# Contiguous key loads, copies on two engines and a join by channel halves in the first stages of a long-convolution kernel

## The chip, the cores and the metric

One Trainium2 chip, one core. The metric is the device time of one execution in microseconds, as the median of several runs of the same program. Engines: TensorE (PE) multiplies matrices into PSUM, VectorE (DVE), ScalarE (ACT) and GpSimd (POOL) work on SBUF (and, here, the first two on PSUM), SyncE (SP) issues most of the DMAs. All arithmetic is in f32.

## The reference

```python
def _A_ref(q, k, v, shift_k, ssm_k, ssm_D):       # S = 2048, D = 448, ks = 4
    k_shift = sum(k_pad[:, t:t + S, :] * shift_k[:, ks - 1 - t] for t in range(ks))
    kv = k_shift * v
    y = causal_conv(kv, ssm_k) + kv * ssm_D       # per channel, 2048 long, by FFT
    return q * y
...
mod = (_silu(c) @ w_mod).reshape(c.shape[0], 6, 1, -1)
sa, ca, ga, sb, cb, gb = ...
h = _layernorm(x) * (1 + ca) + sa
x = x + ga * _A_ref(h, A_k, A_v, A_shift_k, A_ssm_k, A_ssm_D)
h = _layernorm(x) * (1 + cb) + sb
x = x + gb * (sigmoid(h @ w_gate) * (h @ w_up)) @ w_down
```

What matters here is the first half: the short convolution of k with four taps, its product with v, and the long convolution by a Fourier transform written as matrix products. The second half, a gated feed-forward layer, takes the larger part of the time and is not touched.

## The kernel before

The 2048 positions lie as 128 partitions by 16 groups (g), the 448 channels as two halves (h) of 224, or as four blocks (ct) of 112 where the channels lie on the partitions. The order of the instructions on each engine is the order of the program text (a manual schedule). Every engine works off its own queue in order, and waits only for data and for buffers.

**First stage of the kernels** (`stage1_k`, L197 to L207). For half h and load i (four groups), two PSUM tiles (e = 1, then e = 0), each filled by eight matmuls and copied to SBUF (`ak[h]`, 128x896 at a time) by ScalarE. The PSUM tiles come from the tag "t", of which there are two buffers. A few warm-up matmuls go ahead (L572, L573). When half 0 is done, VectorE transposes it in eight steps (`turn`, L181); half 1 goes to DRAM and comes back in another order (`turn_out` L189, `turn_in` L192).

**Second stage of the kernels** (`stage2_k`, L298): eight steps n for half 0, with ScalarE copying out.

**The taps.** `ktl` holds k with the channels on the partitions. Its 16 units (i, ct) each take a tile of 112 x 512. A unit is done in one of three ways: `conv_first` (first product on ScalarE) with three `conv_tap` on VectorE (33 in all); `conv_products` (four products on ScalarE, added by the matmuls that transpose them); or with diagonal matrices on TensorE alone (unit (0,2)). `conv_turn` (L265) transposes a unit into PSUM, in the tags "sa" and "y" (one buffer each), and `conv_mul` (L280) multiplies v by it, in place. The sums of `conv_first` are in the tag "accs", three buffers.

**First stage of kv** (`stage1_v` L209 per group, `stage1_v_half` L223 per half and two groups): matmuls with the same table `zc`, copied to `av[0]` and `av[1]`. Groups 0 to 11 go whole (two copies of 128x448), groups 12 to 15 by halves. For groups 10 and 11, VectorE copies half 1 (L219). When all groups of half 0 are there, VectorE transposes `av[0]` step by step (L183), and the loop `stage2_v` (L318) begins: matmuls, a multiply by the kernels (L332), matmuls back (L349). Between its steps, `beside` (L726) puts the layer norm, the modulation and the second half's kernel stage.

**Loads.** All on SP's queue, in program order. The order is: tables and kernels, `ktl` in 4 + 8 parts (`load_k`, L149), v, the trips of `ak[1]`, then at L683 to L696 two `turn_in`, `mod_load(1)` (L409: two loads of `wmod`, into `spare`, that is the tile `wb`, where groups 8 to 11 of v lie until `stage1_v` has read them), `load_x(0)` and the other `turn_in`. The pool `pk` (with `ktl` and the taps' tiles) is closed at L687, and the pools of x1 and of the "eights" take its place.

Of the kernel before, what the change touches and what calls it, by code (L numbers as in the profile page):

```python
# [10 lines left out]
F32 = mybir.dt.float32  # L11
F32R = mybir.dt.float32r
AF = mybir.ActivationFunctionType
OP = mybir.AluOpType
# [3 lines left out]
P = 128  # L18
C = 224
DT = 112  # L20
NG = 16
# [58 lines left out]
def adaln_conv_glu_kernel(ctx: ExitStack, tc: tile.TileContext, q, kT, v, ssm, shift, dskip,  # L80
                          wgu, wd, cvec, wmod, c1t, w2t, wat, wbt, out):
    nc = tc.nc
    PE, ACT, DVE, POOL = nc.tensor, nc.scalar, nc.vector, nc.gpsimd
# [8 lines left out]
    pk = pk_.enter_context(tc.tile_pool(name="pk", bufs=1, side="right"))  # L92
    ps = ctx.enter_context(tc.tile_pool(name="ps", bufs=1, space=PSUM))
    pd = ctx.enter_context(tc.tile_pool(name="pd", bufs=1, space=bass.MemoryType.DRAM))
    late = {}

    def two(tag, name):

        return ps.tile([P, 2, 512], F32, tag=tag, bufs=2 if tag == "t" else 1, name=name)

    def rows(t):
        return t[:, :, :D]
# [44 lines left out]
        nc.sync.dma_start(xin["v", k], v[:, 2 * k:2 * k + 2])  # L147

    def load_k(ct, part):  # L149
        nc.sync.dma_start(ktl[:, ct, part], kT[:, ct, part])  # L150

    def load_c1(g0, g1):
        nc.sync.dma_start(zc[:, g0:g1], c1t[:, g0:g1])
# [25 lines left out]
    ak = {}  # L179
    
    def turn(a, i):  # L181
        x = a[:, :, i * 28:(i + 1) * 28].rearrange("q p c -> q c p")
        DVE.transpose(x, x)  # L183
# [8 lines left out]
    def turn_in(a, scratch, q, bs=range(4)):  # L192
        x = scratch.rearrange("(b q) p c -> b p q c", b=4)
        for b in bs:
            nc.sync.dma_start(a[32 * b:32 * b + 32, q], x[b, :, q])

    def stage1_k(h, i):  # L197
        x = xin.pop((h, i))
        d = ak[h].rearrange("p (s j) c -> p s (j c)", s=2)
        for e in (1, 0):  # L200
            pt = two("t", f"s1k{h}_{i}_{e}")
            g = 4 * i + 2 * e
            for jj in range(2):
                for s in range(2):
                    r = slice(64 * s, 64 * s + 64)
                    PE.matmul(pt[:, s, jj * C:jj * C + C], zc[r, g + jj], x[r, 2 * e + jj], start=True, stop=True)
            ACT.activation(d[:, :, g * C:(g + 2) * C], rows(pt), AF.Copy)  # L207

    def stage1_v(g):  # L209

        x = xin["v", g // 2][:, g % 2]
        pt = two("t", f"s1v{g}")
        for s in range(2):
            r = slice(64 * s, 64 * s + 64)
            PE.matmul(pt[:, s, :D], zc[r, g], x[r], start=True, stop=True)
        for h in range(2):
            a, y = av[h].rearrange("p (s j) c -> p s j c", s=2)[:, :, g], pt[:, :, h * C:h * C + C]
            if h and g > 9:
                DVE.tensor_copy(a, y)  # L219
            else:  # L220
                ACT.activation(a, y, AF.Copy)

    def stage1_v_half(h, g):  # L223

        pt = two("t", f"s1v{g}_{h}")
        for j in range(2):
            x = xin["v", g // 2][:, j, h * C:h * C + C]
            for s in range(2):
                r = slice(64 * s, 64 * s + 64)
                PE.matmul(pt[:, s, j * C:j * C + C], zc[r, g + j], x[r], start=True, stop=True)  # L230
        d = av[h].rearrange("p (s j) c -> p s (j c)", s=2)
        ACT.activation(d[:, :, g * C:(g + 2) * C], rows(pt), AF.Copy)  # L232

    acc = {}

    def conv_first(i, ct):

        acc[i, ct] = [pk.tile([DT, 4, P], F32, tag="accs", bufs=3, name=f"acc{i}_{ct}")]
        ACT.activation(acc[i, ct][0], ktl[:, ct, 4 * i + 3:4 * i + 7], AF.Copy, scale=sk[:, ct, 0:1])

    def conv_tap(i, ct, tap):
# [6 lines left out]
    def conv_rest(*its):  # L248

        for tap in range(1, 4):  # L250
            for i, ct in its:
                conv_tap(i, ct, tap)

    def conv_products(i, ct):

        acc[i, ct] = []
        for tap in range(4):
            x = ktl[:, ct, 4 * i + 3 - tap:4 * i + 7 - tap]
            a = x if tap == 3 else pk.tile([DT, 4, P], F32, tag="accp", bufs=6, name=f"acp{i}_{tap}")
            ACT.activation(a, x, AF.Copy, scale=sk[:, ct, tap:tap + 1])  # L260
            acc[i, ct].append(a)

    kvs = {}
# [1 line left out]
    def conv_turn(i, *cts):  # L265

        for e in range(2):
            if (i, e) not in kvs:
                kvs[i, e] = two(("sa", "y")[e], f"kv{i}{e}")
            for ct in cts:  # L270
                for g in range(2):
                    y = kvs[i, e][:, g, ct * DT:ct * DT + DT]
                    if (i, ct) not in acc:
                        for tap in range(4):
                            PE.matmul(y, ktl[:, ct, 4 * i + 3 - tap + 2 * e + g], diag[:, tap], start=tap == 0, stop=tap == 3)
                        continue
                    for k, a in enumerate(acc[i, ct]):
                        PE.matmul(y, a[:, 2 * e + g], ident[:DT, :DT], start=k == 0, stop=k == len(acc[i, ct]) - 1, is_transpose=True)

    def conv_mul(i, unit=None):  # L280
        for e in range(2):
            if unit:
                conv_tap(*unit, 2 * e + 1)
                if e == 0:
                    pass
            x = xin["v", 2 * i + e]
            DVE.tensor_mul(x, x, rows(kvs[i, e]))
            if unit and not e:
                conv_tap(*unit, 2)
# [49 lines left out]
    def stage2_back(between=None):  # L339
        h, n, m = products.pop(0)  # L340
        straight = n > (3 if h else 5)
        pt = two("t" if h and n == 7 else "sa", f"sa{h}_{n}")
        for b in range(2):
            if b and between:
                between()
            for ex in range(2):
                r = slice(64 * ex, 64 * ex + 64)
                y = pt[r, b, :D] if not straight else pt[r, b].rearrange("p (j c) -> p j c", c=32)[:, :, :28]
                PE.matmul(y, wa[:, b, r], m[b][:, ex], start=True, stop=True)  # L349
        if straight:  # L350
            y = pt.rearrange("p b (j c) -> p (b j) c", c=32)[:, :, :28]
            DVE.transpose(av[h][:, :, 28 * n:28 * n + 28].rearrange("q p c -> q c p"), y.rearrange("q p c -> q c p"))
            return
        if eights(h, n):
            x = late["pe"].tile([P, 8, DT], F32, name=f"eight{n}")
            late["eights"].append(x)
            x = x.rearrange("p (b j) c -> p b j c", b=2)
        else:
            x = block(av[h], h, n)
        ACT.activation(x, cols4(rows(pt), h, n), AF.Copy)  # L360
# [48 lines left out]
    def mod_load(m):  # L409

        for h in range(2):
            if m != 1:
                wm = quad(*{3: ("m", 4), 4: ("wm", 2), 5: ("wm", 2)}.get(m, ("in", 4)), f"wm{m}{h}")[:DT]
            else:
                wm = spare[:DT, h * 4 * C:(h + 1) * 4 * C].rearrange("p (a c) -> p a c", c=C)
            nc.sync.dma_start(wm, wmod[:, m, h])
            wms[m, h] = wm

# [150 lines left out]
    ordered = tc.manual_schedule()  # L569
    ordered.__enter__()  # L570
    pt = two("y", "warm")
    for i in range(10):  # L572
        PE.matmul(pt[:, 0, :P], ones, ones, start=True, stop=True)  # L573
    for x in (slice(2, 4), slice(0, 2)):
        load_c1(x.start, x.stop)
# [13 lines left out]
    for i in range(4):  # L589
        load_ssm(1, i)  # L590
    nc.sync.dma_start(w2, w2t)
    for ct in (0, 2, 1, 3):
        load_k(ct, ka)
    for h in range(2):
        ak[h] = big.tile([P, 32, C], F32, tag=f"k{h}", name=f"ak{h}")
# [2 lines left out]
    taps = [(i, ct) for i in range(4) for ct in (2, 3)]  # L598
    for k in range(8):
        turn(ak[0], k)  # L600
    for i in range(4):
        stage1_k(1, i)
        load_v(i)
        if i in (1, 3):
            for ct in (0, 2, 1, 3):
                load_k(ct, kb[i // 2])
# [9 lines left out]
    def s1v(*gs):  # L616
        for g in gs:
            stage1_v(g)

    for n in range(8):  # L620
        stage2_k(0, n, "t")
        if n in (0, 1):
            conv_first(0, n)
        if n == 3:
            conv_first(1, 0)
            conv_products(0, 3)
            conv_rest((0, 0), (0, 1))
            conv_turn(0, 2)
        if n == 5:
            conv_first(1, 1)  # L630
            conv_products(1, 2)
            conv_turn(0, 3)
    conv_first(1, 3)
# [42 lines left out]
    for t in (1, 2, 3):  # L676
        conv_tap(3, 3, t)
    conv_turn(3, 2, 0, 1)
    s1v(8, 9)
    conv_turn(3, 3)  # L680
    conv_mul(3)
    s1v(10, 11)
    turn_in(ak[1], kd, slice(0, 8), range(2))  # L683
    mod_load(1)
    if "x" == "y":
        turn_in(ak[1], kd, slice(0, 8), range(2, 4))
    pk_.close()  # L687
    late["px"] = ctx.enter_context(tc.tile_pool(name="px", bufs=1, side="right"))
    late["x1"] = x1 = late["px"].tile([P, NG, D], F32, name="x1")
    pe_ = ExitStack()  # L690
    late["pe"], late["eights"] = pe_.enter_context(tc.tile_pool(name="pe", bufs=1, side="right")), []
    load_x = lambda i: nc.sync.dma_start(x1[:, 4 * i:4 * i + 4], q[:, 4 * i:4 * i + 4])
    load_x(0)
    if "x" != "y":
        turn_in(ak[1], kd, slice(0, 8), range(2, 4))
    turn_in(ak[1], kd, slice(8, 16))  # L696
    for h in range(2):
        for g in (12, 14):
            stage1_v_half(h, g)
        if not h:  # L700
            mod_parts(0, "sa", gbrow)
    pz_.close()
# [722 lines left out]
```

## Time and profile before

| | |
|---|---|
| median of 3 runs | 563.62 us (563.37 to 564.16) |
| profiled execution | 561.75 us |
| its span, first to last instruction | 560.0 us |
| busy: PE / DVE / ACT / POOL | 544.2 / 443.0 / 281.5 / 57.6 us |
| DMA | 107.74 MB, 192 GB/s in the mean |
| granted TensorE clock | 1.0 |

A profile row of the timeline reads: start, time taken, engine, line of the kernel, operation, what it writes <- what it reads, the shape (partitions x elements), how often; in brackets the idle time of the engine ahead of it and what ended it. A row of a stretch gives its length, the busy time of each engine with the number of instructions, the granted clock, the mean busy share of the DMA engines and the rate in GB/s.

### The profile page before, as it was taken

To read this page: it belongs to the slowest core of one execution; us is meant where nothing else is said; L and a number is where in the kernel's file an instruction comes from. 1 tells how busy PE (TensorE), PEld (TensorE's weight loads), DVE (VectorE), ACT (ScalarE), POOL (GpSimd) and SP (SyncE) were. 2 spreads that over 40 slices of the span, in tenths; PEclk is the share of its full clock that TensorE was granted. 3 is DMA by queue.
4 is the path that set the end of the run, shared out by engine and by line. 5 is a ranking of instruction groups with operands and counts; after the bars stand their busy time and mean duration, and the time that the engine had idled before them with its cause. 6 is when DMAs were issued, how large, how long until landed. Compare 5 with 4: busy or idle time off the path is not lost.

```text
span 560.0 us, 7828 instructions
## 1 busy us (share of the span) xinstructions
PE 544.2 (97%) x3010; PEld 415.4 (74%) x3010; DVE 443.0 (79%) x529; ACT 281.5 (50%) x492; POOL 57.6 (10%) x52
## 2 busy tenths in 40 slices
PE   7988899999999999999999999999999999999997
PEld 6564532333577888888888888888888888888886
DVE  0899799989899888898998888885555556879565
ACT  4898688983577586276556452422222222334120
POOL 1000006969500000000000000000000000000000
PEclk9999999999999999999999999999999999999999
DMA  8999899897730408395968295776464662220103
GB/s 278 266 275 391 226 255 288 214 233 159 191 109 0 164 1 322 150 367 187 361 236 307 77 366 162 244 254 240 126 209 135 198 219 105 75 104 8 59 0 132
DMA packets 46953, 107.74 MB, mean 192 GB/s; under 512 B 20034, under 2 KB 25284, under 8 KB 45892
## 3 DMA queue, kind: packets, MB, share of 16 engines
q1 hardware_dynamic: 40468, 82.34, 49.6%
q10 hardware_dynamic: 6448, 24.90, 11.3%
q8 instruction: 24, 0.39, 0.3%
q14 instruction: 13, 0.11, 0.1%
HBM read 70.92 MB, written 35.78 MB: 191 GB/s over the span
## 4 chain that ended last, share of the span: by engine, by line
PE 74%; DMA 10%; DVE 9%; ACT 5%; issue 2%; SPq 0%; DVEq 0%; ACTq 0%
PE d L987 23%; PE b L953 16%; PE c L953 10%; PE a L953 10%; PE gu L1076 4%; DMA kT<-in_kT_dram 4%; PE s2v L328 3%; PE sa L349 2%; PE y L385 2%; DVE av L183 2%; DVE m L332 2%; DMA kdk<-ak 2%; DMA wb<-in_v_dram 1%; DMA inb<-in_ssm_dram 1%; DMA ak<-kdk 1%
## 5 line engine op out<-in xcount | busy, mean ns | idle before, releaser
L987 PE MATMUL d<-wd,h 128*128 128x448 f32 x666 | 144.4, 366 | 0.6 <-DVE wd L547 0.5
L987 PEld LDWEIGHTS d<-wd,h 128*128 128x128 f32 x666 | 124.7, 188 | 13.5 <-DVE wd L547 1.4
L953 PE MATMUL b<-xt,ring 128*128 128x512 f32 x408 | 99.0, 391 | 0.0
L953 PEld LDWEIGHTS b<-xt,ring 128*128 128x128 f32 x408 | 76.5, 188 | 14.9
L1002 DVE TENSOR_TENSOR x<-x,d 128x896 f32<-128x896 f32 x55 | 59.5, 1084 | 16.6 <-PE d L987 16.5
L953 PE MATMUL a<-x,ring 128*128 128x512 f32 x264 | 63.7, 389 | 0.0
L953 PEld LDWEIGHTS a<-x,ring 128*128 128x128 f32 x264 | 49.6, 188 | 10.3
L962 ACT ACTIVATE h<-st 128x512 fp32r<-128x512 f32 x55 | 34.6, 629 | 31.3 <-DVE st L971 19.0
L965 DVE TENSOR_TENSOR h<-st,h 128x512 fp32r<-128x512 f32 x55 | 37.8, 687 | 12.5 <-ACT h L962 12.2
L968 ACT ACTIVATE st<-st 128x512 f32<-128x512 f32 x24 | 15.2, 632 | 63.8 <-DVE st L1313 36.0
L1076 PE MATMUL gu<-x,ring 128*128 128x512 f32 x176 | 42.5, 395 | 0.1
L1267 ACT ACTIVATE st<-st 128x512 f32<-128x512 f32 x12 | 7.6, 631 | 68.0 <-DVE st L1266 68.0
L1076 PEld LDWEIGHTS gu<-x,ring 128*128 128x128 f32 x176 | 32.7, 188 | 7.6 <-issue 0.7
L332 DVE TENSOR_TENSOR m<-s2v,ak 128x896 f32<-128x896 f32 x32 | 33.2, 1078 | 3.9 <-PE s2v L328 2.7
L183 DVE STREAM_TRANSPOSE av<-av 128x896 f32<-128x896 f32 x18 | 33.1, 1874 | 2.4 <-ACT av L232 2.4
L953 PE MATMUL c<-x,ring 128*128 128x512 f32 x144 | 34.8, 390 | 0.0
L934 ACT ACTIVATE ring<-sum 128x512 fp32r<-128x512 f32 x28 | 17.2, 625 | 31.7 <-DVE sum L915 16.8
L328 PE MATMUL s2v<-av,w 64*64 64x448 f32 x256 | 31.8, 546 | 1.0 <-DVE av L183 0.5
L953 PEld LDWEIGHTS c<-x,ring 128*128 128x128 f32 x144 | 27.0, 188 | 5.2
L953 PE MATMUL c<-xt,ring 128*128 128x512 f32 x120 | 29.2, 389 | 0.0
L349 PE MATMUL sa<-m,wa 128*64 128x448 f32 x128 | 27.4, 552 | 0.1
L953 PEld LDWEIGHTS c<-xt,ring 128*128 128x128 f32 x120 | 22.5, 188 | 4.6
(191 smaller groups left out, 778.4 us busy)
## 6 DMA issues: line engine op xcount, KB each, us to landing
fd<-ring ACTq DMA_DIRECT2D x35, 512.0 KB
ring<-fd SPq DMA_DIRECT2D x35, 512.0 KB
wdk<-wd ACTq DMA_DIRECT2D x7, 896.0 KB
wd<-wdk SPq DMA_DIRECT2D x7, 896.0 KB
inb<-in_wgu_dram SPq DMA_DIRECT2D x6, 1024.0 KB
kdk<-ak SPq DMA_DIRECT2D x4, 896.0 KB
ak<-kdk SPq DMA_DIRECT2D x16, 224.0 KB
x<-in_q_dram SPq DMA_DIRECT2D x4, 896.0 KB
```

The source lines that it names most:

```text
L183: DVE.transpose(x, x)
L328: PE.matmul(pts[b][c:c + 64, ex, :D], w2[r:r + 64, ex], x[r:r + 64, b], start=True, stop=True)
L332: DVE.tensor_mul(cols4(m[b], h, n), cols4(rows(pts[b]), h, n), k[:, b].unsqueeze(1).to_broadcast([P, 2, D // w, w]))
L349: PE.matmul(y, wa[:, b, r], m[b][:, ex], start=True, stop=True)
L934: ACT.activation(forms[name, i][:, 0], w_src(name), AF.Copy)
L953: PE.matmul(pt, wh(s, t), x[:, k], start=start and m == 0, stop=stop and m == len(ops) - 1, skip_group_check=True)
L962: ACT.activation(hh, h, AF.Copy)
L965: DVE.tensor_sub(hl, h, hh)
L968: ACT.activation(y[:, 0], y[:, 0], AF.Sigmoid)
L987: PE.matmul(y, h[:, (2 * e + i) * P:(2 * e + i + 1) * P], x, start=m == 0, stop=m == len(ops) - 1)
L1002: DVE.tensor_add(y, y, rows(pt))
L1076: PE.matmul(pt[:, g], plain(q, t)[:, s, g, f * P:f * P + P], xf[xs_[b]][:, k], start=m == 0, stop=m == 10, skip_group_check=True)
```

## The change

- `kT` is laid out in DRAM so that each part that one DMA loads (a block ct, groups 0 to 10, 11 to 14 or 15 to 18) is one contiguous piece; before, each partition's part was a piece of a longer row. The order of the first four blocks is 3, 2, 0, 1 for 0, 2, 1, 3.
- Half 0 of `stage1_k`: the copies of e = 0 go to VectorE. The warm-up has 7 products for 10.
- The four products of unit (0,3) go to GpSimd, issued ahead of everything else there; `conv_first(1,1)` moves ahead from step 5 to step 3; `conv_turn(0,2)` from step 3 to step 4; "accs" has four buffers.
- The join of the taps and of the first stage of kv: `conv_turn(3,3)` stands behind `s1v(8)`, `s1v(9)` after it; groups 10 and 11 go by halves like 12 to 15; the copies on VectorE of half 1 go away; of the six copies by halves, group 12 of half 0 is VectorE's; groups 10 and 14 of half 1 use the PSUM tag "y".
- `mod_load(1)` loads into the tiles that are later the first two "eights", in the place of the closed pool `pk`, and stands behind the closing of that pool.

```diff
     def load_k(ct, part):
-        nc.sync.dma_start(ktl[:, ct, part], kT[:, ct, part])
+        at = DT * ct * (NG + 3) * P
+        w = (part.stop - part.start) * P
+        at += DT * P * part.start
+        nc.sync.dma_start(ktl[:, ct, part].rearrange("p a b -> p (a b)"), kT[at:at + DT * w].rearrange("(p x) -> p x", p=DT))
...
-            ACT.activation(d[:, :, g * C:(g + 2) * C], rows(pt), AF.Copy)
+            if h == 0 and e == 0:
+                DVE.tensor_copy(d[:, :, g * C:(g + 2) * C], rows(pt))
+            else:
+                ACT.activation(d[:, :, g * C:(g + 2) * C], rows(pt), AF.Copy)
...
-            if h and g > 9:
-                DVE.tensor_copy(a, y)
-            else:
-                ACT.activation(a, y, AF.Copy)
+            ACT.activation(a, y, AF.Copy)
-    def stage1_v_half(h, g):
+    def stage1_v_half(h, g, eng, tag):
-        pt = two("t", f"s1v{g}_{h}")
+        pt = two(tag, f"s1v{g}_{h}")
...
-        ACT.activation(d[:, :, g * C:(g + 2) * C], rows(pt), AF.Copy)
+        if eng is DVE:
+            DVE.tensor_copy(d, rows(pt))
+        else:
+            ACT.activation(d, rows(pt), AF.Copy)
...
-        acc[i, ct] = [pk.tile([DT, 4, P], F32, tag="accs", bufs=3, name=f"acc{i}_{ct}")]
+        acc[i, ct] = [pk.tile([DT, 4, P], F32, tag="accs", bufs=4, name=f"acc{i}_{ct}")]
...
-    def conv_products(i, ct):
+    def conv_products(i, ct, eng=ACT):
...
-            ACT.activation(a, x, AF.Copy, scale=sk[:, ct, tap:tap + 1])
+            if eng is POOL:
+                POOL.tensor_scalar(a, x, sk[:, ct, tap:tap + 1], None, op0=OP.mult)
+            else:
+                ACT.activation(a, x, AF.Copy, scale=sk[:, ct, tap:tap + 1])
...
-            x = late["pe"].tile([P, 8, DT], F32, name=f"eight{n}")
+            x = late["pe"].tile([P, 8, DT], F32, tag=f"e{n}", name=f"eight{n}")
...
-                wm = spare[:DT, h * 4 * C:(h + 1) * 4 * C].rearrange("p (a c) -> p a c", c=C)
+                wm = late["pe"].tile([P, 4, C], F32, tag=f"e{h}", name=f"wm1{h}")[:DT]
...
-    for i in range(10):
+    for i in range(7):
         PE.matmul(pt[:, 0, :P], ones, ones, start=True, stop=True)
...
-    for ct in (0, 2, 1, 3):
+    for ct in (3, 2, 0, 1):
         load_k(ct, ka)
...
+    conv_products(0, 3, POOL)
...
         if n == 3:
             conv_first(1, 0)
-            conv_products(0, 3)
+            conv_first(1, 1)
             conv_rest((0, 0), (0, 1))
+        if n == 4:
             conv_turn(0, 2)
         if n == 5:
-            conv_first(1, 1)
             conv_products(1, 2)
             conv_turn(0, 3)
...
     conv_turn(3, 2, 0, 1)
-    s1v(8, 9)
+    s1v(8)
     conv_turn(3, 3)
+    s1v(9)
     conv_mul(3)
-    s1v(10, 11)
     turn_in(ak[1], kd, slice(0, 8), range(2))
-    mod_load(1)
...
+    mod_load(1)
     load_x(0)
...
     for h in range(2):
-        for g in (12, 14):
-            stage1_v_half(h, g)
+        for g in (10, 12, 14):
+            stage1_v_half(h, g, DVE if (h, g) == (0, 12) else ACT, "y" if h and g != 12 else "t")
         if not h:
             mod_parts(0, "sa", gbrow)
...
+    kt = np.concatenate([kt[:, ct, s].reshape(-1) for ct in range(4) for s in (slice(0, 11), slice(11, 15), slice(15, NG + 3))])
```

More of the change, by code (lines that the diff above doesn't have):

```diff
@@ L230, in stage1_v_half @@
                 PE.matmul(pt[:, s, j * C:j * C + C], zc[r, g + j], x[r], start=True, stop=True)
-        d = av[h].rearrange("p (s j) c -> p s (j c)", s=2)
-        ACT.activation(d[:, :, g * C:(g + 2) * C], rows(pt), AF.Copy)
+        d = av[h].rearrange("p (s j) c -> p s (j c)", s=2)[:, :, g * C:(g + 2) * C]
+        if eng is DVE:
+            DVE.tensor_copy(d, rows(pt))
+        else:
+            ACT.activation(d, rows(pt), AF.Copy)
     acc = {}
     def conv_first(i, ct):
-        acc[i, ct] = [pk.tile([DT, 4, P], F32, tag="accs", bufs=3, name=f"acc{i}_{ct}")]
+        acc[i, ct] = [pk.tile([DT, 4, P], F32, tag="accs", bufs=4, name=f"acc{i}_{ct}")]
         ACT.activation(acc[i, ct][0], ktl[:, ct, 4 * i + 3:4 * i + 7], AF.Copy, scale=sk[:, ct, 0:1])
@@ L678, in adaln_conv_glu_kernel @@
     conv_turn(3, 2, 0, 1)
-    s1v(8, 9)
+    s1v(8)
     conv_turn(3, 3)
+    s1v(9)
     conv_mul(3)
-    s1v(10, 11)
     turn_in(ak[1], kd, slice(0, 8), range(2))
-    mod_load(1)
-    if "x" == "y":
-        turn_in(ak[1], kd, slice(0, 8), range(2, 4))
     pk_.close()
@@ L692, in adaln_conv_glu_kernel @@
     load_x = lambda i: nc.sync.dma_start(x1[:, 4 * i:4 * i + 4], q[:, 4 * i:4 * i + 4])
+    mod_load(1)
     load_x(0)
-    if "x" != "y":
-        turn_in(ak[1], kd, slice(0, 8), range(2, 4))
+    turn_in(ak[1], kd, slice(0, 8), range(2, 4))
     turn_in(ak[1], kd, slice(8, 16))
     for h in range(2):
-        for g in (12, 14):
-            stage1_v_half(h, g)
+        for g in (10, 12, 14):
+            stage1_v_half(h, g, DVE if (h, g) == (0, 12) else ACT, "y" if h and g != 12 else "t")
         if not h:
```

## The prediction

> **What bounds the kernel now.** I read the page first, for the span and for the engine that the chain of work runs through, and then the busy time by stretches.
>
> ```profile
> span 560.0 us, 7828 instructions
> ...
> PE 74%; DMA 10%; DVE 9%; ACT 5%; issue 2%; SPq 0%; DVEq 0%; ACTq 0%
> ```
>
> The profiled run took 561.75 us: 1.75 us lie outside the span of 560.0. The median of the three runs shown is 563.62, so 1.87 above the profiled one; I sum against the profile and carry the difference over.
>
> ```profile
> core 0: us, PE busy (x) PEld busy (x) DVE busy (x) ACT busy (x) POOL busy (x), PEclk, DMA share, GB/s
> 16.40:30.40 14.00, 12.95 (x112) 7.85 (x109) 13.97 (x9) 12.79 (x16) 0.00 (x0) 1.00 1.03 251
> 30.40:60.00 29.60, 25.43 (x189) 16.01 (x189) 28.23 (x39) 25.18 (x45) 0.00 (x0) 1.00 1.01 320
> 60.00:70.00 10.00, 8.67 (x76) 5.03 (x74) 6.50 (x6) 6.87 (x11) 0.00 (x0) 1.00 0.82 225
> 70.00:120.00 50.00, 48.33 (x351) 15.21 (x345) 48.42 (x43) 44.37 (x107) 31.22 (x24) 1.00 1.03 240
> 120.00:178.00 58.00, 57.32 (x447) 34.12 (x445) 51.52 (x70) 35.53 (x61) 23.30 (x16) 1.00 0.56 143
> 178.00:560.00 382.00, 378.33 (x1761) 326.01 (x1759) 293.09 (x359) 148.38 (x245) 0.00 (x0) 1.00 0.50 176
> ```
>
> The change touches only the first 70 us; after 178 TensorE is full, and from 16.4 to 60 VectorE is (13.97 of 14.00, 28.23 of 29.60). The loose place is 60 to 70: there VectorE works 6.50 of 10 and nobody is full. From 70 to 178 VectorE or TensorE is full again. So what the change wins or loses up to 70 should reach the end nearly whole, and it can win it in three places: the start of VectorE's work at 16.4, the 1.37 us that VectorE idles from 30.4 to 60, and the join at 60 to 70. Here is VectorE in order of time; the bracket is the idle time ahead and what ended it:
>
> ```profile
> 16.43 13.97 DVE L183 STREAM_TRANSPOSE ak<-ak 128x896 f32<-128x896 f32 x8 [9.69 <-ACT ak L207]
> ...
> 35.34 2.08 DVE L244 SCALAR_TENSOR_TENSOR acc<-kT,sk,acc 112x512 f32<-112x512 f32 x3 [0.36 <-ACT acc L239]
> ...
> 52.64 2.08 DVE L287 TENSOR_TENSOR wb<-wb,kv 128x896 f32<-128x896 f32 x2 [0.38 <-PE kv L278]
> ...
> 58.86 0.75 DVE L244 SCALAR_TENSOR_TENSOR kT<-kT,sk,acc 112x512 f32<-112x512 f32 x1
> 61.07 2.08 DVE L287 TENSOR_TENSOR inb<-inb,kv 128x896 f32<-128x896 f32 x2 [1.46 <-DMA ak<-kdk]
> 63.08 1.15 DVE L219 COPY av<-s1v 128x448 f32<-128x448 f32 x2
> 66.65 3.60 DVE L183 STREAM_TRANSPOSE av<-av 128x896 f32<-128x896 f32 x2 [2.43 <-ACT av L232]
> 70.41 2.09 DVE L332 TENSOR_TENSOR m<-s2v,ak 128x896 f32<-128x896 f32 x2 [0.16 <-PE s2v L328]
> ...
> 74.47 2.09 DVE L332 TENSOR_TENSOR m<-s2v,ak 128x896 f32<-128x896 f32 x2
> ```
>
> **The first stage's copies on two engines, and three warm-up products fewer.**
>
> ```profile
> 9.52 1.78 PE L206 MATMUL s1k<-inb,zc 64*128 64x224 f32 x16 [0.58 <-ACT ak L207]
> 11.55 1.84 PE L206 MATMUL s1k<-inb,zc 64*128 64x224 f32 x16 [0.25 <-ACT ak L207]
> 13.59 1.84 PE L206 MATMUL s1k<-inb,zc 64*128 64x224 f32 x16 [0.20 <-ACT ak L207]
> ```
>
> ```profile
> L207 ACT ACTIVATE ak<-s1k x16: 912/917/921, 8.2 to 23.7; 128x896 f32<-128x896 f32 x16
> ```
>
> ```profile
> L332 DVE TENSOR_TENSOR m<-s2v,ak x32: 1036/1080/1107, 70.4 to 142.8; 128x896 f32<-128x896 f32 x32
> ```
>
> There are two PSUM buffers, one for e=1 and one for e=0. Each goes round: eight matmuls, copy, free. The rounds start 2.04 us apart (11.55 to 13.59), of which the copy is 0.92 and the rest 1.12. Four of the eight copies of half 0 go to VectorE. No row shows a VectorE copy of 128x896 from PSUM; two of 448 take 1.15 (L219) and a multiply of that size out of PSUM takes 1.08, which I take. The round of the e=0 buffer then lasts 1.12 + 1.08 = 2.20, longer, not shorter. From the group at 9.52: its matmuls end at 11.30, copies at 11.35, 13.55 and 15.75, the last done at 16.83. The eight transposes need all of it and start at about 16.85 in place of 16.43: **+0.4 us**. The opposite bound: the last block of kernels lands at 13.01 (below), sixteen matmuls later it is 14.79, with a copy 15.87: -0.55.
>
> ```profile
> 5.47 7.54 DMA inb<-in_ssm_dram
> ...
> 13.02 10.96 DMA kT<-in_kT_dram
> ```
>
> The warm-up goes from 20 to 14 matmuls.
>
> ```profile
> 1.98 4.63 PE L573 MATMUL warm<-ones 128*128 128x128 f32 x20 [1.98 <-DVE ones L162]
> 6.54 2.39 PE L206 MATMUL s1k<-inb,zc 64*128 64x224 f32 x16
> ```
>
> They cost 0.23 each, so the first group can start 1.4 earlier, but the second group at 9.52 waits for its load; I cost it at nothing. If the clock rises later for it, that is the third rival. [...]
>
> **The tap stage, 30 to 60.** Unit (0,3)'s four products leave ScalarE for GpSimd, conv_first(1,1) moves ahead, and there are four buffers of sums.
>
> ```profile
> 29.91 1.95 ACT L260 ACTIVATE acp<-kT,sk 112x512 f32<-112x512 f32 x3
> ```
>
> ```profile
> L509 POOL TENSOR_SCALAR G<-x,rstd,nmr x16: 523/533/542, 88.0 to 125.8; 128x224 f32<-128x224 f32 x16
> ```
>
> ScalarE is rid of four products of 0.65, 2.6 us, but VectorE keeps its 33 taps and eight multiplies, so that is worth only the stall of 0.36 at 35.34, where it waited for just that first sum (1,1): **-0.36**. GpSimd pays 512/224 x 0.53 = 1.22 per product, 4.9 in all; it is idle there, TensorE reads the products only after 33, and the block that they need is now first in the queue, where today's first lands by some 21 (the second at 13.02 + 10.96 = 23.98, a block of 616 KB at the 232 GB/s below being 2.7 us), so they are done by 26. The stall of 0.38 at 52.64 hangs on TensorE work of the same order as before; I leave it (0 to -0.38). Net at 60: about 0.
>
> **Unbroken key blocks.**
>
> ```profile
> 18.40:28.40 10.00, 9.06 (x78) 4.46 (x75) 10.00 (x6) 9.11 (x12) 0.00 (x0) 1.00 1.02 232
> 42.40:56.00 13.60, 11.92 (x67) 6.12 (x67) 13.06 (x19) 12.51 (x24) 0.00 (x0) 1.00 1.02 391
> ```
>
> While the key blocks land the queues are full at 232 GB/s; later, equally full, they move 391. The blocks are 4.26 MB (4 x 616 + 8 x 224 KB). At the second rate they'd take 11 us in place of 18: up to 7 us of queue. But the wait that this could shorten does not exist: no tap and no multiply before 60 waits for a DMA, and the 1.37 us of idle bound what VectorE can gain at all. The 1.46 "<-DMA ak<-kdk" at 61.07 is a multiply of v and PSUM; that DMA feeds neither. **0**, whether the blocks are faster or not. The chain of waits, which puts kT on it, only follows the last arrival.
>
> **The join, 60 to 70.** ScalarE's row first, then TensorE's.
>
> ```profile
> 59.99 1.85 ACT L221 ACTIVATE av<-s1v 128x448 f32<-128x448 f32 x4 [1.85 <-PE s1v L215]
> ```
>
> ```profile
> 58.92 1.77 PE L215 MATMUL s1v<-wb,zc 64*128 64x448 f32 x8
> 60.62 0.60 PE L278 MATMUL kv<-ident,kT 112*128 112x112 f32 x4
> 61.16 1.77 PE L215 MATMUL s1v<-wb,zc 64*128 64x448 f32 x8
> 63.74 1.78 PE L230 MATMUL s1v<-inb,zc 64*128 64x224 f32 x16 [0.81 <-DVE av L219]
> 65.46 0.96 PE L427 MATMUL mod<-inb,scb 112*32 112x224 f32 x16
> 66.35 1.78 PE L230 MATMUL s1v<-inb,zc 64*128 64x224 f32 x16
> ```
>
> The last tap ends at 59.61, but its transposes stand behind s1v(8) and s1v(9) until 60.62; the multiplies follow 0.45 later. Then s1v(10), s1v(11) and two VectorE copies behind the multiplies hold the PSUM buffers until 63.65. After the change: transposes behind s1v(8) alone, 59.80; multiplies 60.25 and 61.25, done 62.33 (now 63.15). s1v(9) at 60.2, its two copies on ScalarE (0.46 apart, 0.55 long) until 62.2. Group 10 of half 0 is copied 62.1 to 63.0. Group 12 takes the buffer free at 62.2: matmuls (0.91) to 63.15, VectorE copy to 64.3, beside the others. Group 14 takes the buffer free at 63.0: matmuls to 63.95, ScalarE to 65.0. So the first transpose of av starts at 65.1, not 66.65: **-1.5**. But half 1 now has three groups ahead of s2v on TensorE: mod 63.95 to 64.9, group 10 in "y" to 65.8 (copied by 66.7), group 12 to 66.7, group 14 in "y" once it is free, 66.75 to 67.65. s2v starts at 67.6, where now it is 68.65 (the transpose at 66.65 + 1.86 and ScalarE's copies): -1.05. Its sixteen matmuls no longer wait for a buffer in their middle: 1.7, and the multiply starts at 69.3 for 70.41; after its pair (2.05) and a transpose (1.75) the next pair stands at 73.1 for 74.47: **-1.35**.
>
> mod_load(1) leaves wb's spare room, where it waits for groups 8 to 11, for the area freed with the last tap.
>
> ```profile
> 60.73 2.56 SPq L416 DMA_DIRECT2D wb<-in_wmod_dram  x2
> 63.39 0.38 SPq L692 DMA_DIRECT2D x<-in_q_dram  x1
> ```
>
> All of SP's queue behind it (x and 14 transfers of ak) leaves some 2.4 us earlier, at 61.0; that keeps the loads ahead of an engine chain that comes 1.35 earlier, and I count no gain of its own. Sum: +0.4 - 0.36 - 1.35 = **-1.3 us**: 560.45 as a profiled run, 562.3 as a median.
>
> **The rivals.** (a) *More*: the first stage comes out near its lower bound (0.95 better than I take) and the stall of 0.38 goes as well: -2.6, 561.0. For it: ScalarE is relieved by four copies and four products. Against: the buffers' rounds above. (b) *Taken back*: the array stays slow into the group at 9.52. The group at 6.54, slow for about half its time, took 0.61 longer than the next; all slow would be +1.2, passed on by the chain of buffers to the transposes: -0.1, 563.5. For it speaks the shorter warm-up, against it that TensorE has work from 1.98 to some 8 without a hole of even 0.5. [...] (c) *Slower*: blocks 0 and 1 of the keys now come last of four, and VectorE's taps at 30.8 need block 1. At today's pace of 2.7 per block from 18.4 the fourth lands at 29.3, its first product (about 0.7 on ScalarE) stands at 30.0, and the tap that needs it comes at 31.2: in time by 1.2. If the unbroken form were slower, it decides from some 10% on; at half as slow again the fourth lands at 34.5, the tap comes at 35.2 and waits 4.0 us, and the sum is +2.7: 566.3. Against it: nothing in a contiguous read suggests it.
>
> **How the numbers follow.** About 0.2% (1.1 us) can be told from no change. My forecast has 0.53, with its own range 561.3 to 563.2; (a) 0.18, (b) 0.20, (c) 0.09. Of the forecast's 0.53 some 0.37 lie below 562.5. So faster 0.55, same 0.36, slower 0.09. The range 560.6 to 563.8 takes in (a) and (b) and leaves out (c).
>
> **What would show it.** First transposes of ak at 16.8 (right) or 16.0 (rival a); no wait at the taps of (1,1); taps (3,3) ending near 59.6; first transpose of av near 65.1 and second pair of m near 73.1; key blocks moving at over 300 GB/s with VectorE's taps unmoved; the s1k matmuls from 9.5 in 1.8 per sixteen, or near 3 (b). The prediction is wrong if VectorE's work from 30 to 60 gets shorter or longer than 29 us, or if the 1.35 us won at 74 are not found again at 178.

## The result, and the profile after

| | before | after |
|---|---|---|
| median | 563.56 us (561.51 to 566.00, 20 runs) | 565.31 us (562.64 to 568.23, 20 runs) |
| ratio, 95% interval | | 1.0041 [1.0028, 1.0054] |
| profiled execution | 561.75 us, span 560.0 | 563.53 us, span 561.7 |

The change makes the kernel slower by 0.4%; 562.3 was forecast, and the range ended at 563.8. Between the two profiled executions lie 1.78 us, and 3.1 between the measured 563.53 and the 560.45 that the sum gave for a profiled run. Ratios leave out runs over 1.5% above the fastest of the same kernel, which below concerns six of the twelve of e1_order_0132 alone.

Of the page of after, the span and the chain of waits:

```profile
span 561.7 us, 7835 instructions
...
PE 64%; DVE 5%; ACT 2%; issue 1%; DVEq 0%; ACTq 0%
```

The DMAs have gone from the chain (10% before), although, as will be seen, the time was lost to a DMA: the chain follows only what came last. The stretches that the prediction began with, of after:

```profile
16.40:30.40 14.00, 10.63 (x92) 5.70 (x88) 13.89 (x9) 10.40 (x13) 6.22 (x4) 1.00 1.03 250
30.40:60.00 29.60, 25.85 (x192) 16.71 (x193) 27.31 (x38) 24.90 (x43) 0.00 (x0) 1.00 0.97 309
60.00:70.00 10.00, 9.41 (x86) 6.39 (x84) 7.38 (x8) 6.05 (x10) 0.00 (x0) 1.00 0.85 237
```

VectorE (third figure) idles 2.3 us of the 29.6 instead of 1.4; the DMAs of the first stretch, most of them kT's, move 250 GB/s, as before (251). VectorE in order of time, the rows that answer to those of before:

```profile
15.85 1.09 DVE L211 COPY ak<-s1k 128x896 f32<-128x896 f32 x1 [1.13 <-PE s1k L209]
17.05 13.92 DVE L186 STREAM_TRANSPOSE ak<-ak 128x896 f32<-128x896 f32 x8
...
34.82 2.72 DVE L250 SCALAR_TENSOR_TENSOR acc<-kT,sk,acc 112x512 f32<-112x512 f32 x4
...
40.62 2.09 DVE L296 TENSOR_TENSOR inb<-inb,kv 128x896 f32<-128x896 f32 x2 [1.75 <-PE kv L287]
...
60.83 0.75 DVE L250 SCALAR_TENSOR_TENSOR kT<-kT,sk,acc 112x512 f32<-112x512 f32 x1
62.29 2.08 DVE L296 TENSOR_TENSOR inb<-inb,kv 128x896 f32<-128x896 f32 x2 [0.71 <-PE kv L287]
...
67.31 3.61 DVE L186 STREAM_TRANSPOSE av<-av 128x896 f32<-128x896 f32 x2 [0.67 <-ACT av L238]
71.98 2.09 DVE L341 TENSOR_TENSOR m<-s2v,ak 128x896 f32<-128x896 f32 x2 [1.06 <-PE s2v L337]
...
75.78 2.04 DVE L341 TENSOR_TENSOR m<-s2v,ak 128x896 f32<-128x896 f32 x2
```

Against before: the transposes start 0.62 later (17.05 for 16.43), the stall of 0.36 inside the taps of (1,1) is gone (four taps without a bracket at 34.82), a wait of 1.75 for kv stands where before the first multiply came at 38.66 without one, so the last tap is 1.97 late (60.83 for 58.86). The join gives back 0.66: at the second pair of m after is 1.31 late (75.78 for 74.47). Where does the new wait come from? ScalarE and TensorE of after, from the timeline:

```profile
26.98 0.72 ACT L245 ACTIVATE acc<-kT,sk 112x512 f32<-112x512 f32 x1 [0.84 <-DMA kT<-in_kT_dram]
28.56 0.98 PE L305 MATMUL s2k<-ak,w 64*64 64x448 f32 x8 [1.38 <-ACT ak L311]
29.47 0.72 ACT L245 ACTIVATE acc<-kT,sk 112x512 f32<-112x512 f32 x1 [0.96 <-DMA kT<-in_kT_dram]
31.05 0.98 PE L305 MATMUL s2k<-ak,w 64*64 64x448 f32 x8 [1.51 <-ACT ak L311]
31.96 3.83 PE L284 MATMUL kv<-arow,kT 112*128 112x112 f32 x32
...
39.98 0.98 PE L287 MATMUL kv<-ident,kT 112*128 112x112 f32 x8
```

Read from the DMA onwards: the first products of blocks 0 and 1 (L245) wait for their loads. The copies of the kernels' second stage (L311) stand behind them in ScalarE's queue and start at 27.61 and 30.10; TensorE, whose s2k matmuls need the buffers that those copies free, idles 1.38 and 1.51; its 32 matmuls of unit (0,2) start at 31.96 (28.17 before), and the last transposes of group 0 at 39.98 (36.94). VectorE's taps, which I had watched, came in time; its multiply, which waits for TensorE, did not.

### The profile page after: what moved, and what is told of

It is laid out like the page before. It is cut to its first block, busy times and chain, and to the rows that moved or that the text cites. A ratio compares the mean times of both kernels' runs of the same rounds, so it can differ in the third digit from the quotient of the medians.

```text
span 561.7 us, 7835 instructions
## 1 busy us (share of the span) xinstructions
PE 544.2 (97%) x3012; PEld 414.8 (74%) x3012; DVE 447.3 (80%) x532; ACT 276.1 (49%) x483; POOL 63.8 (11%) x56
## 4 chain that ended last, share of the span: by engine, by line
PE 64%; DVE 5%; ACT 2%; issue 1%; DVEq 0%; ACTq 0%
PE d L994 23%; PE b L960 16%; PE c L960 10%; PE a L960 10%; PE gu L1083 4%; PE pt L878 1%; DVE h L972 1%; ACT xn L860 0%; DVE xn L858 0%; ACT full L883 0%; DVE x L1009 0%; DVE wd L556 0%; DVE ring L576 0%; DVE st L476 0%; DVE ring L945 0%
## 5 line engine op out<-in xcount | busy, mean ns | idle before, releaser
L978 DVE TENSOR_TENSOR st<-st 128x512 f32<-128x512 f32 x24 | 16.6, 692 | 11.9 <-ACT st L975 11.7
```

The lines of the kernel that those rows point to most:

```text
L978: DVE.tensor_mul(y[:, 0], y[:, 0], y[:, 1])
```

## The experiments

All ratios are to the kernel before, run beside it on the same chip.

**The order alone** (e3_order_alone):

```diff
-    for ct in (0, 2, 1, 3):
+    for ct in (3, 2, 0, 1):
```

> The kernel before with one edit: the first four key blocks in the order 3, 2, 0, 1. Theory (order): ScalarE waits for blocks 0 and 1 until about 26.7 and 29.3, its copies of the second stage and TensorE's share come some 2 us later, the first multiply near 40.5 or later; 1.5 to 3 us above before (ratio 1.003 to 1.005). Rival (first stage): no difference, since this edit leaves the first stage alone.

Measured: 565.06 us, ratio 1.0050 [1.0028, 1.0072]. The order alone, in the old layout, costs as much as the whole change. Its profiled run is the slowest of the twelve (569.10, mean granted clock 0.991); the three whose granted clock was 1.000 took 561.63, 562.98 and 563.14. So the wait by itself costs up to some 1.5 us, and the rest of the 2.7 us between the medians (562.32 for before in that batch) comes with a lowered clock. Its timeline:

```profile
28.02 0.72 ACT L239 ACTIVATE acc<-kT,sk 112x512 f32<-112x512 f32 x1 [2.35 <-DMA kT<-in_kT_dram]
...
29.59 1.77 PE L296 MATMUL s2k<-ak,w 64*64 64x448 f32 x8 [2.90 <-ACT ak L302]
31.30 6.07 PE L275 MATMUL kv<-arow,kT 112*128 112x112 f32 x32
...
40.72 2.08 DVE L244 SCALAR_TENSOR_TENSOR acc<-kT,sk,acc 112x512 f32<-112x512 f32 x3 [5.53 <-ACT acc L239]
```

The wait of 2.35 on ScalarE becomes 2.90 on TensorE, and then more is lost than was waited for: behind that idle time the same 32 matmuls take 6.07 instead of 3.83 (the granted clock is 0.50 from 30 to 36), and VectorE waits 5.53.

**Two other orders.** With 0, 1, 3, 2 (e1_order_0132) the products on GpSimd stay; with 0, 2, 1, 3 (e2_order_act) they return to ScalarE, since their block would come last.

```diff
-    for ct in (3, 2, 0, 1):
+    for ct in (0, 1, 3, 2):      # e1_order_0132
+    for ct in (0, 2, 1, 3):      # e2_order_act
...
-    conv_products(0, 3, POOL)    # e2_order_act, and there at step 3:
+            conv_products(0, 3)
```

> The changed kernel with one edit: the first four key blocks are loaded in the order 0, 1, 3, 2 in place of 3, 2, 0, 1. Theory (order): in the changed kernel the first products of units (0,0) and (0,1) wait on ScalarE for the blocks that come last (0.84 and 0.96 us), the second stage's copies stand behind them, TensorE loses 1.38 and 1.51, and VectorE idles 1.75 at its first multiply. With blocks 0 and 1 first these waits go: first multiply by v near 38.9 in place of 40.62, and about 1.8 us less than the changed kernel, that is some 0.4 under the kernel before (ratio near 0.999). Rival (first stage): the transposes that start 0.62 later are what the end is late by; then the time stays 0.6 us or more above before. Rival (GpSimd): its four products now fall beside VectorE's taps (27 to 33 us); if the two engines block each other, taps and products get longer by some us and the time stays above before by over 1 us.

Measured: 569.25 us, in two groups, four runs at 561.1 to 561.9 and eight at 568.4 to 571.2. The ratio, 1.0027 [0.9989, 1.0065], says little; the trace is of the upper group. The waits of ScalarE are gone, and another stands in their place. VectorE from the timeline, and then the view of the tile that GpSimd writes (shortest, median and longest instruction in ns, then the first and last start):

```profile
30.89 2.70 DVE L250 SCALAR_TENSOR_TENSOR acc<-kT,sk,acc 112x512 f32<-112x512 f32 x4
...
37.48 1.42 DVE L250 SCALAR_TENSOR_TENSOR kT<-kT,sk,acc 112x512 f32<-112x512 f32 x2
47.35 2.09 DVE L296 TENSOR_TENSOR inb<-inb,kv 128x896 f32<-128x896 f32 x2 [8.45 <-PE kv L287]
```

```profile
L267 POOL TENSOR_SCALAR acp<-kT,sk x3: 1556/1562/8967, 28.3 to 31.4; 112x512 f32<-112x512 f32 x3
```

Two products take 1.56 each, as in after, beside VectorE's transposes. The third starts at 31.4, half a microsecond behind the first tap, and takes 8.97: it ends at 40.4, 1.5 (its own length) behind the last of twelve taps without a gap (38.9). TensorE waits for it, VectorE for TensorE. The four runs near 561.5 had a granted clock of 0.999 or 1.000, the eight others 0.990 to 0.994; what the four did differently has no trace and stays open.

> The changed kernel with the old order of key blocks (0, 2, 1, 3) and the four products of unit (0,3) back on ScalarE, behind the first product of (1,1). All else stays changed. Theory (order): first multiply near 38.9, no wait on ScalarE for a key block ahead of the second stage's copies, ratio to before near 0.999. Rival (first stage): 0.6 us or more above before. If GpSimd's products cost anything by themselves, this one is faster than the one with the order 0, 1, 3, 2.

Measured: 561.93 us, ratio 0.9993 [0.9981, 1.0005]. Undoing the order (with the products) takes away the loss, as expected. Its profiled run took 563.07 and shows something else, a slow array at the group near 9.5 as in rival (b) (which the prediction's first mention calls the third):

```profile
7.35 1.03 PE L209 MATMUL s1k<-inb,zc 64*128 64x224 f32 x8 [0.40 <-DVE inb L143]
9.86 4.22 PE L209 MATMUL s1k<-inb,zc 64*128 64x224 f32 x24 [1.49 <-DMA inb<-in_ssm_dram]
```

After seven warm-up products and 1.49 of idle time 24 matmuls take 4.22, where in after 16 from 9.59 took 1.78; the granted clock is 1.00 from 8 to 10 and 0.51 from 10 to 12, and the transposes start at 18.77. So the array did not stay slow from the start: the clock was up and fell.

**The join alone** (e4_join_alone): the hunks of the diff for `stage1_v` and `stage1_v_half`, for the room of `mod_load(1)` and for the join; all else as before.

> The kernel before with the join alone: the transposes of (3,3) behind s1v(8), groups 10 to 14 by halves with one copy on VectorE, the tag y for two of them, mod_load(1) into its new room. The prediction's term was -1.35 us; the traces of before and after, from the last tap (+1.97) to the second pair of m (+1.31), give only about -0.7. Expected -0.7 us, ratio 0.9988; if the prediction's term was right and something else took it, 0.9976.

Measured: 562.47 us, ratio 1.0000 [0.9976, 1.0023], which tells nothing; its runs too fall in two groups (560.7 to 561.4, 562.2 to 563.7, one at 566.6). In the trace the second pair of m starts at 73.61, 0.86 ahead of before, and the span is 559.0: the gain is there in that trace, smaller than forecast, and what hides it in the median is taken up below.

**The layout alone, and another source.** e5_contig has the hunks of `load_k` and `kt` alone; e6_src_v fills the same tiles from another tensor:

```diff
-        nc.sync.dma_start(ktl[:, ct, part], kT[:, ct, part])
+        src = v[:DT].rearrange("p a b -> p (a b)")
+        n = (part.stop - part.start) * P
+        nc.sync.dma_start(ktl[:, ct, part].rearrange("p a b -> p (a b)"), src[:, 1024 * ct:1024 * ct + n])
```

> The kernel before with kT contiguous per part and nothing else. Theory (the layout doesn't speed the blocks): 18.4 to 28.4 still moves 230 to 250 GB/s at a full DMA share, the four blocks land within 0.5 us of where they land before, ratio 1.000 within 0.001. Rival (the step on record that counted 7 us of queue as possible): over 300 GB/s there, blocks landing 2 us and more earlier, and still ratio 1.000, since no tap waits for a block in the order 0, 2, 1, 3.

> The kernel before, with ktl filled from rows of v in place of kT (so the keys are not the right ones; shapes, bytes and destination are the same). Theory A (the place read is what is slow): 18.4 to 28.4 moves 350 GB/s or more, as v's own loads do. Theory B (the destination or the 112 partitions are what is slow): 230 to 250 GB/s as with kT.

Measured: 561.70 us, ratio 0.9989 [0.9974, 1.0003], and 561.82 in one run. The same stretch of e5_contig, and then of e6_src_v (last figure GB/s):

```profile
18.40:28.40 10.00, 9.05 (x78) 4.63 (x77) 10.00 (x7) 9.14 (x11) 0.00 (x0) 1.00 1.02 280
```

```profile
18.40:28.40 10.00, 9.05 (x77) 4.63 (x77) 10.00 (x7) 8.74 (x11) 0.00 (x0) 1.00 1.02 245
```

For e5_contig neither expectation held to the letter: 280 GB/s in this stretch, more than the 250 of the one and less than the 300 of the other. But the first three blocks are complete at 20.8, 24.5 and 27.0 in the trace, where before has 21.3, 24.0 and 26.7, so nothing comes earlier that anyone waits for. With v as the source, whose parts are pieces of longer rows too, it is 245, so it is not the tensor read; and with kT in one piece per part (280 here, 246 in after) it stays below the 391 of the later stretch, so it is not the broken rows alone. The tiles written have 112 partitions in all three; whether that is the cause was not tried.

**The parts that gain** (e7_best): the join, four buffers of sums and `conv_first(1,1)` at step 3; everything else as before.

> The kernel before with three parts of the change: the join, four buffers of tap sums, conv_first(1,1) two steps earlier; old load order, ScalarE's products, ten warm-up products and ScalarE's copies stay. Theory: the stall of 0.36 at the first tap of (1,1) goes and the join gives 0.65 to 0.86: 1.0 to 1.2 us, ratio 0.998; transposes of ak start at 16.4, taps end 0.36 earlier than before. Rival (the gains are taken back after 74): ratio 1.000.

Measured: 560.66 us (560.55 to 561.40), ratio 0.9959 [0.9946, 0.9973], 2.3 us instead of the 1.2 expected. Its profiled run is only 0.9 faster than that of before (560.83 for 561.75). So the median gained 1.4 that this pair of traces does not show. e9_taps_alone leaves out the join and keeps the two edits of the taps:

```diff
-... tag="accs", bufs=3
+... tag="accs", bufs=4
             conv_first(1, 0)
+            conv_first(1, 1)
             conv_products(0, 3)
...
         if n == 5:
-            conv_first(1, 1)
```

> The kernel before with four buffers of tap sums and conv_first(1,1) two steps earlier, and nothing else. Theory: the stall of 0.36 at the first tap of (1,1) goes and no wait takes its place (with the old load order ScalarE's products of (0,3) no longer stand ahead of that sum); ratio 0.9994 from the stall alone. If it also spares TensorE the idle time behind which its clock falls in some executions, the runs about 1.8 us above the fastest get rare, and the ratio is 0.997 to 0.998. Rival: no change, 1.000.

Measured: 561.22 us, ratio 0.9976 [0.9964, 0.9987], all nine runs at 561.0 to 562.1. To see what before does in its upper group, it was run once more:

> The kernel before, unchanged, for a second trace of it. Its runs lie in two groups, near 561.6 and near 563.3. Theory: the upper group are executions in which TensorE's clock falls to half once for some 3.5 us. If this execution takes over 563, its rows show a stretch of 3 to 4 us at a granted clock near 0.5 before 62 us, behind an idle time of TensorE of over 1 us, and VectorE waiting for kv behind it; if it takes under 562, the clock is 1.00 throughout as in the first trace. Rival: over 563 with the clock at 1.00 throughout (then the two groups have another cause, a DMA or the time outside the span).

Measured: 563.25 us, and so a trace of the upper group. TensorE in the first trace of before, and then in this one:

```profile
36.94 0.98 PE L278 MATMUL kv<-ident,kT 112*128 112x112 f32 x8
39.89 0.48 PE L278 MATMUL kv<-ident,acp 112*128 112x112 f32 x3 [1.96 <-DVE inb L287]
...
41.06 0.45 PE L278 MATMUL kv<-ident,acp 112*128 112x112 f32 x3
```

```profile
36.98 0.98 PE L278 MATMUL kv<-ident,kT 112*128 112x112 f32 x8
39.93 0.48 PE L278 MATMUL kv<-ident,acp 112*128 112x112 f32 x3 [1.96 <-DVE inb L287]
...
41.59 0.77 PE L278 MATMUL kv<-ident,acp 112*128 112x112 f32 x3
```

From the group at 9.5 to here the two executions are the same to 0.05 us, the idle time of 1.96 too. Behind it the clock falls in one and not in the other (three matmuls take 0.77 instead of 0.45, until about 44), and the last tap ends 1.66 later. That is about the distance between the groups, and so most of the 1.87 that lay between the profiled run and the median in the prediction.

The mean granted clock of each of these runs is on record, and such falls can be counted in it: profiled runs without one read 0.999 or 1.000, with one stretch of 3.4 us 0.995 to 0.997, with two 0.994. By that count before had a fall in 17 of 35, 19 of 23 and 16 of 26 runs of the three batches; its runs without one lie from 561.4 to 562.3, but for one at 563.45. e7_best had none in six runs, e9_taps_alone none in nine, e4_join_alone had seven in twelve, e5_contig four in ten.

**Two parts put back into e7_best.** e10_best_warm7 has `range(7)` for the warm-up; e11_best_copies has the hunk of `stage1_k`.

> e7_best with seven warm-up products in place of ten, and nothing else. Theory (the third rival on record, in a part of the executions): TensorE idles longer than 1 us ahead of the group at 9.5, its clock falls to half for some 3.4 us in those executions, which then take about 1.5 to 1.8 us more: runs in two groups, 560.6 and 562.2, median ratio above that of e7_best by 0.001 to 0.003. Rival (no effect): ratio 0.996 and one group of runs, as e7_best.

Measured: 561.00 us (560.03 to 562.56), ratio 0.9970 [0.9959, 0.9980]: not to be told from e7_best, and no clear groups; two of its twelve runs show a fall (clock 0.996). In its trace the idle time ahead of the second load is 1.41, and the clock stays up.

> e7_best with the four copies of e = 0 of half 0 on VectorE, and nothing else (ten warm-up products). Theory: each pair of rounds takes 2.21 in place of 2.04; the transposes start 7.46 behind the start of the group at 9.3 in place of 6.92: +0.55 us, ratio above that of e7_best by 0.001. Rival (lower bound on record: the copies on two engines shorten the stage): 0.5 us earlier, ratio below that of e7_best by 0.001.

Measured: 562.74 us, ratio 0.9993 [0.9978, 1.0009], 0.0034 above e7_best where 0.001 was expected; five runs at 560.7 to 561.2, seven, just those with a fall, at 562.6 to 564.7. Its trace shows both halves of the price:

```profile
9.26 1.78 PE L206 MATMUL s1k<-inb,zc 64*128 64x224 f32 x16 [0.96 <-DMA inb<-in_ssm_dram]
...
16.72 13.97 DVE L183 STREAM_TRANSPOSE ak<-ak 128x896 f32<-128x896 f32 x8
...
39.73 0.48 PE L281 MATMUL kv<-ident,acp 112*128 112x112 f32 x3 [1.78 <-ACT acc L242]
...
41.25 0.77 PE L281 MATMUL kv<-ident,acp 112*128 112x112 f32 x3
```

From the group at 9.26 to the transposes it is 7.46, as in after (9.59 to 17.05); with all copies on ScalarE it is 6.92 in e7_best (9.28 to 16.20): 0.54 for the copies. The other half comes from TensorE: VectorE's multiply comes 0.48 later than in e7_best (38.46 for 37.98) and TensorE's transposes ahead of it 0.37 earlier (36.97 for 37.34), so TensorE's idle time at 39 grows to 1.78, from 0.89 in e7_best:

```profile
37.98 2.08 DVE L287 TENSOR_TENSOR inb<-inb,kv 128x896 f32<-128x896 f32 x2
...
39.21 0.48 PE L278 MATMUL kv<-ident,acp 112*128 112x112 f32 x3 [0.89 <-DVE inb L287]
...
73.06 2.06 DVE L332 TENSOR_TENSOR m<-s2v,ak 128x896 f32<-128x896 f32 x2
```

Put together, the idle time of TensorE at 39 to 40 goes with the groups: 1.96 or 1.97 in before, e4_join_alone and e5_contig and 1.78 in e11_best_copies, all with an upper group; 1.34 in e9_taps_alone and 0.89 in e7_best, without one. (1.54 in e10_best_warm7 lies between, and so do its runs.) It is not the only place: e2_order_act and e8_warm10, with 1.02 and 0.89 there, have three and five runs of twelve with a fall, and in their traces it lies elsewhere, at 10.0 and at 57.8.

**All of the change but order and GpSimd, with ten warm-up products** (e8_warm10; e2_order_act with `range(10)`).

> The changed kernel with the old load order and (0,3)'s products on ScalarE, as in e2_order_act, and ten warm-up products in place of seven. Theory (the shorter warm-up leaves TensorE idle so long ahead of the group at 9.5 that in some executions its clock falls to half, as it did in e2_order_act's profiled run behind an idle time of 1.49): here the idle time is under 1, the clock stays at 1.00 from 8 to 16, transposes of ak start at 17.0, and the ratio is 0.998 for e2_order_act's 0.9993. Rival (the fall was one execution's chance and the warm-up does nothing): ratio 0.9993 and the same scatter.

Measured: 562.45 us, ratio 0.9987 [0.9974, 1.0001], not to be told from e2_order_act. The transposes start at 16.64, and the clock is 1.00 from 8 to 16, as expected; but in this execution the clock falls at another place:

```profile
54.81 0.31 PE L287 MATMUL kv<-ident,acp 112*128 112x112 f32 x1
55.28 0.32 PE L287 MATMUL kv<-ident,acp 112*128 112x112 f32 x1 [0.15 <-ACT acp L269]
55.89 0.32 PE L287 MATMUL kv<-ident,acp 112*128 112x112 f32 x1 [0.29 <-ACT acp L269]
56.64 0.32 PE L287 MATMUL kv<-ident,kT 112*128 112x112 f32 x1 [0.44 <-ACT kT L269]
...
57.91 0.77 PE L287 MATMUL kv<-ident,acp 112*128 112x112 f32 x3
```

Here no single idle time is long; four matmuls in 2.1 us, a pattern that before has at the same place, stand ahead of this fall. So the warm-up's own effect stays open: one fall was seen behind the shorter one, and none in the trace of e10_best_warm7 behind nearly the same idle time; and five of twelve runs with ten products had a fall, three of twelve with seven.

## Why the prediction was wrong

The step that failed is the one on the **unbroken key blocks**, at 0, and the working of rival (c), which bounded it. Its pace was nearly right (2.5 to 2.6 per block for 2.7; the fourth is there by 29.47, 29.3 was forecast). "In time by 1.2" was worked out for the tap on VectorE. The wait falls earlier, on ScalarE (until 26.98 and 29.47; VectorE's first tap starts at 30.88), and it delays not what VectorE needs next but what is queued behind: copies, s2k, `conv_turn`, multiply. That "no tap and no multiply before 60 waits for a DMA" held for the old order only, and the change moved just those two blocks from first and third to third and fourth. So (c)'s mechanism came with no slower block at all; "from some 10% on" was wrong, and 0.09 was too little. Shown: with the order alone the loss is there, with the order (and the products that hang on it) undone it is gone.

In terms of the sum, on the profiled runs (3.1 us; that of after is the slowest of its four runs without a fall of the clock, 562.64 to 563.53):

- **First stage**: +0.62 for +0.4. The mechanism was right, a slower round of the e=0 buffer, at 2.22 (13.63 to 15.85) where 2.20 was worked out; measured from the group's own start it is 0.55. The rest is that the group starts at 9.59 for 9.52.
- **Taps**: -0.36, as forecast. Its effect on the clock, worth more than that in the median of e9_taps_alone, was not foreseen.
- **Key blocks**: +1.75 for 0. Over 300 GB/s was named as a sign; it stayed at 246 in the same ten microseconds (232 before).
- **GpSimd's products**: done at 28.3 instead of 26, at 1.57 each and not 1.22; hidden by the load order that was chosen for them; with the order 0, 1, 3, 2 the third took 8.97.
- **Join**: -0.66 for -1.35, counted from the end of the taps. The multiplies are right to 0.1 (62.29; 60.25 and the 1.97 of delay give 62.22). The transposes of av come 0.2 late and s2v 0.6: the first groups by halves wait 0.32 for ScalarE's copies of s1v(9), and the third of half 1 waits 0.26 for its buffer "y". I had both without a wait.
- **The loads behind `mod_load(1)`**: it leaves at 62.59; 61.0 and the 1.97 give 62.97. No gain had been counted.
- **Afterwards**: from 1.31 at 75.78 to 1.7 at the end of the span, +0.4. Late by 1.35 at the multiply of 109.45, after loses another 0.3 by 178; this was not followed up. In e7_best the same stretch takes from the 1.41 gained at 73.06 down to 1.0: there the multiplies at 103 and 107 wait 0.67 and 0.52 for s2v (0.28 and 0.29 before). So that the gains are found again at 178 held only for about 70% of them.

These make +0.2, +1.75, +0.7 and +0.4 beside the forecast, 3.05 of the 3.1.

Rival (b), 0.20: the array was slow there in one traced execution (e2_order_act; it did not stay slow but fell, the clock having been up from 8 to 10), where from the group at 9.86 the 7.46 would have led to 17.32 and the transposes start at 18.77: 1.45, for the 1.2 put on it. In the profiled run of after it does not happen (16 matmuls from 9.59 in 1.78). Carrying the 1.87 between the profiled run and the median over as a constant was a step without ground: it hangs on the share of executions in which the clock falls, and the change alters that share. The runs of after spread over 5.6 us: sixteen of the twenty show a fall by their granted clock, nine of them two or more (0.990 to 0.994), and the four without one lie some 1 us above such runs of before, less than the 1.78 of the traced pair. Where in after the clock falls was not traced; its idle times of 1.38 and 1.51 at 28 to 31 are possible places, which is not shown. The 0.61 by which the sixteen matmuls from 6.54 took longer than later ones (2.39 for 1.78) rested on one execution: in e12_before_again the same sixteen took 1.78.

## What to carry to other kernels

When loads are put in another order, look for the first instruction on any engine that needs each load, and then at what is queued behind that instruction; the engine that seems to need the data may be in time while the queue of another is not. A part whose ends are priced in one trace should also be read for the idle times that it leaves on TensorE: here the edit that took a stall of 0.36 from VectorE also cut an idle time of TensorE from 1.96 to 1.34, and gained 1.3 us in the median (e9_taps_alone). And what GpSimd's work costs should be read beside what VectorE does at that time: in the trace of e1_order_0132 the same product took 1.56 us beside VectorE's transposes and 8.97 beside its taps.

## What the runs showed of the hardware

**A clock that falls in some executions.** Behind idle times of 1.49 (e2_order_act), 1.78 (e11_best_copies), 1.96 (e12_before_again) and 1.97 us (e3_order_alone, at 45.26) TensorE's granted clock went to one half, for some 3.4 us as the shares of its two-microsecond stretches add up (0.65 and 0.50 from 40 to 44 in e12_before_again); in the course of 2.90 in e3_order_alone and 4.49 in e1_order_0132 it did so for 6.8 us. Behind the same 1.96 in another execution (the first trace of before), behind 1.97 in e4_join_alone and e5_contig, and behind 1.51 (after), 1.41 (e10_best_warm7) and 1.25 (e12_before_again, at 9.56), it did not. A fall of 3.4 us cost 1.45 us (e2_order_act) and 1.66 us (e12_before_again).

Worked out from the shares in the same way, the clock of e3_order_alone changes at 29.20, 36.04, 46.28 and 49.68, so 6.84, 10.24 and 3.40 us apart: twice, three times and once the 3.41 of the fall in e12_before_again. Here are the 3.42 us of e12_before_again ahead of its fall and the stretch of the fall, and then the same place in the first trace of before, where the clock stays up:

```profile
37.17:40.59 3.42, 1.46 (x15) 1.27 (x15) 3.42 (x5) 3.39 (x6) 0.00 (x0) 1.00 1.06 222
40.59:44.00 3.41, 3.41 (x22) 3.13 (x19) 3.41 (x6) 0.79 (x2) 0.00 (x0) 0.50 1.03 302
```

```profile
37.13:40.55 3.42, 1.46 (x15) 1.27 (x15) 3.42 (x5) 3.39 (x6) 0.00 (x0) 1.00 1.08 246
```

TensorE is busy 1.46 us of 3.42 in both, and the clock falls behind one of them. In the 3.4 us ahead of the seven falls traced it was busy for 0.18 of the time (e1_order_0132), 0.26 and 0.42 (e3_order_alone), 0.43 (e12_before_again), 0.45 (e2_order_act), 0.48 (e11_best_copies) and 0.72 (e8_warm10). So a low share stands ahead of six of the seven, but it does not decide by itself; what sets the two executions apart is not shown, and no run here tries it.

**GpSimd beside VectorE.** The product of 8.97 us in e1_order_0132 starts half a microsecond behind the first of VectorE's twelve taps (31.4, 30.89) and ends 1.5 behind the last (40.4, 38.9). The taps kept their pace (four in 2.70 us; 2.68 in after, where GpSimd is done at 28.3, before they start). The two products ahead of it, beside VectorE's transposes, and the one behind it, from 40.42, when VectorE waits, took 1.56 each. That the taps held the product up is how this one traced execution reads; by what means, no run shows.
